# Attention and experts on one core: loads and stores handed out in pieces at two places of each step, instead of one whole load at its head

## The chip, the cores and the metric

The kernel runs on one core of one Trainium2 chip. The metric is the device time of one execution in microseconds (us). Of the core, five engines matter: PE (TensorE, matrix products and transposes), PEld (its weight loads), DVE (VectorE), ACT (ScalarE), POOL (GpSimd) and SP (SyncE), which in this part of the kernel only issues transfers. Transfers run on 16 DMA engines, which the core's queues share.

## The reference

An attention over 8 batches of 8 heads, with 512 local and 32 global positions; its output is the input of a layer of 8 experts.

```python
k_all = concat([k_g, k_l], axis=2); v_all = concat([v_g, v_l], axis=2)
out_g = sm(scale * q_g @ k_all.T) @ v_all                   # 32 global queries see all
s_ll = where(|i - j| <= 32, scale * q_l @ k_l.T, -1e9)      # 512 local queries: a band
s_lg = scale * q_l @ k_g.T                                  # ... and the 32 global keys
out_l = sm(concat([s_lg, s_ll], -1)) @ concat([v_g, v_l], 2)
x = concat([out_g, out_l], 2) as (8*544 rows, 512)
logits = x @ w_gate; tokens are given to 8 experts of 544 places each, best logits first
out[tokens of e] = max(x @ w1[e], 0) @ w2[e]
```

All is in 32-bit floats.

## The kernel before, in words

The program has three parts. Attention runs to about 226 us, the choice of the experts to about 252 us, and the eight experts fill the rest. Only the attention's transfers are touched.

**Units.** Attention is cut into 80 units. A batch has eight `Local` units (two heads, half of the sequence) and two `Glob` units (four heads' global queries), in the order of four local, one global, four local, one global; the last batch has its global units earlier. A unit has four parts, each for one or two engines: `a` are the score products on PE (S, line 139, 16 PE instructions in a unit, or line 204); `e` is the masked maximum on DVE (p, line 146, and nm, line 148) and the exponential on ACT (line 151, or 219 to 225); `c` are the transposes of the weights on PE (T, line 156 or 233) and their copy out of PSUM, by ACT (line 258) or DVE (line 260); `d` are the products with the values on PE (O, line 168 or 243) and the division on DVE (lines 171 to 176, or 246 to 250). The gate's transposes and products (lines 266, 272, 281) of the batch before are strewn between.

**Steps.** The loop runs `i` from -2 to 82. Step `i` holds `a` and `e` of unit `i+2`, `c` of unit `i` and `d` of unit `i-2`. An even step goes a, c, gate, e, d; an odd step d, c, gate, a, e. The schedule is written out by hand: each engine runs its instructions in the order in which the code calls for them.

**Transfers.** There are 32 pairs of heads. A pair has a `qk` tile (queries and keys, 704 KB, 5 buffers) and a `vw` tile (the values by windows, 1040 KB, 6 buffers). When a `qk` tile has landed, POOL spreads its queries into a `qz` tile with two copies (line 91). A batch stores four pieces of its local output, `xs`, of 128x512 floats (256 KB each), and two small ones, `xg`, of its global output (line 251). All of these are issued by SP, which does so in program order: an issue that waits holds back what stands behind it. One more transfer, the table `cf` of 512 KB for the choice of the experts, is issued by POOL, behind some of its copies.

**When a transfer goes.** At the head of each step one whole load is issued: a `vw` if fewer values than keys have been called for, else the next `qk` if it is no more than three pairs ahead. `paced` ties it to the newest `nm` of DVE (line 148), so that it goes no earlier than that. The stores of a batch's `xs` are queued in `stores`, and one goes at the end of each step, tied to nothing but its data. Beside that a load waits for its buffer.

**The program's own instructions** are moved by queue 8 of the DMA engines, which the profile lists as "instruction".

Of the kernel before, what the change touches and what calls it, by code (L numbers as in the profile page):

```python
# [65 lines left out]
def attention(ctx, tc, A, consts, xd, ident, L, nbatch, rt=None):  # L66
# [8 lines left out]

    seen, stores = [], []

    def paced(ins):
        if seen:
            tc.add_manual_dep(ins.ins if hasattr(ins, "ins") else ins, seen[-1], AFTER, reason="pace")  # L80

    def load_qk(b, p):
        t = ld.tile([128, QW + KW], F32, name="qk", bufs=5)
        z = qz[(b * NP + p) % NZ]
        paced(nc.sync.dma_start(t, A["qk"][b, p]))
        q, qk[b, p] = t[:, :QW], t[:, QW:]

        def spread(eng):
            for h in range(2):
                r = slice(64 * h, 64 * h + 64)  # L90
                eng.tensor_copy(z[r, :, h, :], q[r].rearrange("p (j i) -> p j i", i=32))  # L91
        return spread

    def load_v(b, p):
        t = ld.tile([128, 2, NW, D + 1], F32, name="vw", bufs=6)
        paced(nc.sync.dma_start(t.rearrange("p h w d -> p (h w d)"), A["vw"][b, p]))
        vw[b, p] = t

# [19 lines left out]
    spread1 = load_qk(0, 1)  # L118
    load_v(0, 0)
    nc.sync.dma_start(wg.rearrange("p a b -> p (a b)"), A["wg"])  # L120
    load_qk(0, 2)(nc.gpsimd)
    load_v(0, 1)

    class Local:
# [3 lines left out]
        def a(s):  # L128
# [6 lines left out]
            for c in range(NB):  # L135
                for r in range(2):
                    j = 8 * s.u + 2 * c + r
                    k0 = 32 * ((3 * j + 1) // 2)
                    nc.tensor.matmul(st[64 * r:64 * r + 64, c, :], z[:, j].rearrange("p h i -> p (h i)"),  # L139
                                     kw[:, k0:k0 + 128], start=True, stop=True)  # L140
            s.st = st

        def e(s):
            st, nm = s.st, s.nm
            for c in range(NB):
                nc.vector.tensor_tensor_reduce(s.p[:, c, :], st[:, c, :], mask[:, 4 * s.u + c, :], 1.0, -BIG,  # L146
                                               ALU.add, ALU.max, nm[:, c:c + 1])
            mark = nc.vector.tensor_scalar(nm, nm, -SCALE, None, op0=ALU.mult)  # L148
            seen.append(mark.ins.name if hasattr(mark, "ins") else mark.name)
            for c in range(NB):  # L150
                nc.scalar.activation(s.p[:, c, :], s.p[:, c, :], AF.Exp, bias=nm[:, c:c + 1], scale=SCALE)  # L151

        def c(s):
            t = ps.tile([128, NB, 128], F32, name="T", bufs=3)
            for c in range(NB):
                nc.tensor.transpose(t[:, c, :], s.p[:, c, :], ident)  # L156
            s.pt = wk.tile([128, NB, 128], F32, name="pt", bufs=4)
            evac(s.pt, t, bool(s.u) if s.b == nbatch - 1 and s.q == NP - 1 else None)

        def d(s):  # L160
            b, q, u = s.b, s.q, s.u
            o = ps.tile([128, 2, 2, D + 1], F32, name="O", bufs=2)
            for h in range(2):
                for k in range(2):
                    for r in range(4):
                        jj = 4 * k + r
                        lo = 64 * (jj % 2) + 32 * h
                        nc.tensor.matmul(o[32 * r:32 * r + 32, k, h, :], s.pt[:, jj // 2, lo:lo + 32],  # L168
                                         vw[b, q][:, h, 8 * u + jj, :], start=True, stop=True)
            ls = wk.tile([128, 2, 2], F32, name="ls", bufs=4)  # L170
# [8 lines left out]
    def store(b):  # L179
        for k in range(NB):  # L180
            stores.append(lambda k=k: nc.sync.dma_start(
                ap_of(xd, (b * S + SG + 128 * k) * DM, [[DM, 128], [1, DM]]), xs[b][:, k]))

    class Glob:
# [3 lines left out]
        def a(s):  # L188
# [3 lines left out]
            for part in range(2):  # L192
                for r in range(2):
# [7 lines left out]
                    else:  # L201
                        mv = t[:, 32:64]
                        dd = s.sb[64 * r:64 * r + 64]
                    nc.tensor.matmul(dd, z, mv, start=True, stop=True)  # L204

# [22 lines left out]
        def c(s):  # L228
            s.pt = wk.tile([128, 6, 128], F32, name="pgt", bufs=3)
            for lo, n in ((0, 4), (4, 2)):  # L230
                t = ps.tile([128, NB, 128], F32, name="T", bufs=3)
                for k in range(n):
                    nc.tensor.transpose(t[:, k, :], s.p[:, lo + k, :], ident)  # L233
                evac(s.pt[:, lo:lo + n], t[:, :n])

        def d(s):
# [3 lines left out]
            for k in range(6):  # L240
                for r in range(4):
                    h = 4 * g + r
                    nc.tensor.matmul(o[32 * r:32 * r + 32, :], s.pt[:, k, 32 * r:32 * r + 32],  # L243
                                     vw[b, h // 2][:, h % 2, 3 * k + 1 if k < 5 else 14, 0:D],
                                     start=(k == 0), stop=(k == 5))
            nc.vector.tensor_reduce(m[:, 6:7], m[:, 3:6], axis=AX.X, op=ALU.add)
# [117 lines left out]
    for b in range(nbatch):  # L364
# [9 lines left out]
        else:  # L374
            for k, f in enumerate(lo):
                (wide if k == 4 else turns).setdefault(s0 + 1 + (k if b == nbatch - 2 else GS[k]), []).append(f)
            if gl:
                extra.setdefault(s0 + 2, []).append(lambda b=b: load_gx(b // 4))
                for k, f in enumerate(gl):
                    (wide if k == 4 else turns).setdefault(s0 + 11 + k, []).append(f)  # L380
    nl = [3, 2]

    def pairidx(u):
        if isinstance(u, Local):
            return u.b * NP + u.q
        return u.b * NP + 2 * u.g + 1

# [3 lines left out]
    for i in range(-LA, nu + 3):  # L391
        if rt and i == 2:
            rt.load()
        if rt and i == 12:
            rt.prepare()
        if i + LA < nu:
            if i >= 0 and nl[1] < nl[0]:
                load_v(*P[nl[1]])
                nl[1] += 1
            elif nl[0] < len(P) and nl[0] <= pairidx(units[i + LA]) + 3:  # L400
                load_qk(*P[nl[0]])(nc.gpsimd)
                nl[0] += 1
        even = i % 2 == 0
# [6 lines left out]
        if 0 <= i < nu:  # L410
            units[i].c()
        for f in turns.get(i, []):
            f()
        if not even and i + LA < nu:
            units[i + LA].a()
        if i + LA < nu:
            units[i + LA].e()
            if i + LA == 0:
                spread1(nc.vector)
        if even and 2 <= i <= nu + 1:  # L420
            units[i - 2].d()
            for f in wide.get(i, []):
                f()
        for f in extra.get(i, []):
            f()
        while stores:
            stores.pop(0)()
            if i < nu - 1:
                break
        if rt and i >= nu - 8:  # L430
# [803 lines left out]
```

## Time and profile before

| | |
|---|---|
| median of three runs | 703.04 us (699.8, 703.04 and 705.38) |
| the profiled execution: its own time | 701.61 us |
| its span in the profile | 699.8 us |
| granted clock of PE, mean of the span | 0.973 |
| PE busy in the span | 656.6 us (94%), 8182 instructions, and as many weight loads |
| DVE, ACT, POOL busy | 73%, 44%, 23% |

The profile is of one execution; its parts are told in the span's own time, which begins at 0. A row that gives a wait names what the engine waited for; "issue" there means time in which it waited for nothing that the profile shows. The granted clock is a share of full speed: 1.00 is 2.4 GHz, and 0.5 is 1.2 GHz.

### The profile page before, as it was taken

Reading aid. Unit: us, or ns where it says so; the run is one execution under the profiler, and the core shown is the slowest. Engines: PE = TensorE matmul, PEld = TensorE weight load, DVE = VectorE, ACT = ScalarE, POOL = GpSimd, SP = SyncE. Lnnn points to the kernel's source line nnn. Section 1 sums busy time; section 2 is a strip of 40 time slices with the busy share of each in tenths; the row PEclk is TensorE's granted clock in tenths of the full one; section 3 lists DMA queues with packets and bytes.
Section 4 is the critical chain, followed back from the end, with each engine's and each line's share of the span. In section 5 each row is a group of like instructions: output and inputs, shape, how many; then the busy total and the mean of one; then the engine's idle time right before and its main releaser. Section 6 shows DMA issues by size and latency. Waiting matters only on the chain.

```text
span 699.8 us, 20349 instructions
## 1 busy us (share of the span) xinstructions
PE 656.6 (94%) x8182; PEld 554.1 (79%) x8182; DVE 512.1 (73%) x2073; ACT 305.6 (44%) x839; POOL 164.2 (23%) x202
## 2 busy tenths in 40 slices
PE   8989999899999259999999999999999999999996
PEld 6767886787876148978978978987987997988985
DVE  4888887888887787888997987988977871631510
ACT  4647665666665013424433332433442451642411
POOL 5231221321210041052142124132132133312011
PEclk9999999999999559999999999999999999999998
DMA  9989998998942043054144224424324324622001
GB/s 364 420 289 349 337 315 320 309 307 314 346 144 100 2 154 151 4 191 177 29 160 166 89 101 140 177 81 154 137 69 164 138 69 166 195 71 104 16 20 45
DMA packets 27102, 120.45 MB, mean 172 GB/s; under 512 B 5632, under 2 KB 5888, under 8 KB 18816
## 3 DMA queue, kind: packets, MB, share of 16 engines
q1 hardware_dynamic: 16368, 66.72, 26.2%
q0 software_dynamic: 10640, 52.44, 21.5%
q8 instruction: 64, 1.05, 0.6%
q14 instruction: 30, 0.25, 0.1%
HBM read 101.32 MB, written 17.83 MB: 170 GB/s over the span
## 4 chain that ended last, share of the span: by engine, by line
PE 85%; DVE 10%; issue 2%; ACT 1%; DMA 1%; POOLq 0%; SPq 0%; DVEq 0%; ACTq 0%
PE H L1076 27%; PE Y L1102 25%; PE S L139 8%; PE T L156 4%; PE O L168 4%; PE R L564 3%; PE Y L1092 2%; PE H L902 2%; PE S L204 2%; PE T L233 2%; PE O L243 2%; PE T L266 2%; DVE p L146 1%; DVE r_G L489 1%; DVE w1l L489 1%
## 5 line engine op out<-in xcount | busy, mean ns | idle before, releaser
L1076 PE MATMUL H<-xh,w1h 128*128 128x272 f32 (+2 forms) x512 | 149.2, 292 | 1.2 <-ACT xh L875 0.8
L1076 PE MATMUL H<-xh,w1l 128*128 128x272 f32 (+2 forms) x512 | 149.6, 293 | 0.3 <-DVE w1l L489 0.3
L1076 PE MATMUL H<-xl,w1h 128*128 128x272 f32 (+2 forms) x512 | 148.6, 291 | 0.2 <-DVE xl L489 0.2
L151 ACT ACTIVATE p<-p,nm 128x128 f32<-128x128 f32 x256 | 81.7, 391 | 63.9 <-DVE nm L148 50.7
L1102 PE MATMUL Y<-w2h,hh 128*128 128x512 f32 x256 | 104.1, 407 | 0.0
L1102 PE MATMUL Y<-w2h,hl 128*128 128x512 f32 x256 | 103.3, 403 | 0.0
L1102 PE MATMUL Y<-w2l,hh 128*128 128x512 f32 x256 | 103.3, 403 | 0.0
L1079 ACT ACTIVATE hh<-H 128x272 fp32r<-128x272 f32 (+2 forms) x128 | 50.8, 397 | 114.4 <-PE H L1076 106.9
L1076 PEld LDWEIGHTS H<-xh,w1h 128*128 128x128 f32 x512 | 96.7, 189 | 2.2 <-ACT xh L875 1.1
L1076 PEld LDWEIGHTS H<-xl,w1h 128*128 128x128 f32 x512 | 96.3, 189 | 0.8 <-DVE xl L489 0.6
L1076 PEld LDWEIGHTS H<-xh,w1l 128*128 128x128 f32 x512 | 96.6, 189 | 0.4 <-DVE w1l L489 0.4
L91 POOL COPY qz<-qk 64x544 f32<-64x544 f32 x60 | 38.2, 636 | 146.0 <-DMA qk<-in_qk_dram 82.9
L139 PE MATMUL S<-qk,qz 128*64 128x128 f32 x1024 | 68.3, 283 | 4.4 <-issue 3.2
L489 DVE SCALAR_TENSOR_TENSOR hl<-H,hh 128x272 fp32r<-128x272 f32 (+2 forms) x128 | 55.0, 435 | 20.7 <-ACT h L1081 13.2
L146 DVE CUSTOM_DVE_ANT_0 p<-S,mask 128x128 f32<-128x128 f32 x256 | 58.8, 286 | 12.7 <-PE S L139 11.7
L139 PEld LDWEIGHTS S<-qk,qz 128*64 128x64 f32 x1024 | 57.4, 141 | 11.0 <-issue 8.4
L489 DVE TENSOR_TENSOR w2l<-w2r,w2h 128x512 fp32r<-128x512 f32 x64 | 41.9, 686 | 30.5 <-ACT w2h L875 30.0
L862 POOL DMA_INDIRECT xg<-xd,idx x40 | 39.7, 992 | 101.5 <-DVE idx L489 41.0
L1038 ACT ACTIVATE y<-Y 128x512 f32<-128x512 f32 x32 | 19.1, 598 | 94.7 <-PE Y L1102 79.8
L1102 PEld LDWEIGHTS Y<-w2h,hh 128*128 128x128 f32 x256 | 48.3, 189 | 10.3 <-issue 1.6
L1102 PEld LDWEIGHTS Y<-w2h,hl 128*128 128x128 f32 x256 | 48.3, 189 | 9.2
L1102 PEld LDWEIGHTS Y<-w2l,hh 128*128 128x128 f32 x256 | 48.4, 189 | 8.9
(185 smaller groups left out, 1139.7 us busy)
## 6 DMA issues: line engine op xcount, KB each, us to landing
vw<-in_vw_dram SPq DMA_DIRECT2D x32, 1040.0 KB
qk<-in_qk_dram SPq DMA_DIRECT2D x32, 704.0 KB
xd<-xs SPq DMA_DIRECT2D x32, 256.0 KB
xg<-xd,idx POOLq DMA_INDIRECT x40
mask<-in_mask_dram SPq DMA_DIRECT2D x1, 512.0 KB
cf<-in_cf_dram POOLq DMA_DIRECT2D x1, 512.0 KB
xd<-xg SPq DMA_DIRECT2D x16, 32.0 KB
gx<-xd POOLq DMA_DIRECT2D x8, 64.0 KB
```

The lines of the kernel that those rows point to most:

```text
L91: eng.tensor_copy(z[r, :, h, :], q[r].rearrange("p (j i) -> p j i", i=32))
L139: nc.tensor.matmul(st[64 * r:64 * r + 64, c, :], z[:, j].rearrange("p h i -> p (h i)"), kw[:, k0:k0 + 128], start=True, stop=True)
L146: nc.vector.tensor_tensor_reduce(s.p[:, c, :], st[:, c, :], mask[:, 4 * s.u + c, :], 1.0, -BIG, ALU.add, ALU.max, nm[:, c:c + 1])
L151: nc.scalar.activation(s.p[:, c, :], s.p[:, c, :], AF.Exp, bias=nm[:, c:c + 1], scale=SCALE)
L156: nc.tensor.transpose(t[:, c, :], s.p[:, c, :], ident)
L168: nc.tensor.matmul(o[32 * r:32 * r + 32, k, h, :], s.pt[:, jj // 2, lo:lo + 32], vw[b, q][:, h, 8 * u + jj, :], start=True, stop=True)
L489: return op(*args, **kw)
L564: s.nc.tensor.matmul(out, *args, **kw)
L862: nc.gpsimd.indirect_dma_start(out=dst, out_offset=None, in_=src, element_offset=off, in_offset=bass.IndirectOffsetOnAxis(ap=idx, axis=0))
L1076: nc.tensor.matmul(p, w[d][:, fs], x[:, d, q], start=(k == 0), stop=(k == 11))
L1079: nc.scalar.activation(hh[:, f, q], p, AF.Relu)
L1102: nc.tensor.matmul(p, h[:, f, q], w[f], start=(f + k == 0), stop=(f + k == 9))
```

## The change

`move` takes the place of `paced`: a transfer is tied to `mark`, the newest product or transpose of PE at the place where it is called for. Stores go through `move` as well. `slot` issues at most one piece. It is called twice in each step from the first: right behind `c`, and at the end of PE's part of the step (behind `a` in an odd one, behind `d` in an even one). It takes the next `qk` if, by its own reckoning of buffers, one is free and the pair is needed no later than the next values (with a lead that favours keys by four units), else a store if more than two are queued or no values can go, else one half of a `vw`. The values so go in halves of 520 KB, one head each. Before the first step the same loads go as before, the values in two halves, and one more `qk` at the very start of the loop. A batch's two `xg` stores stand where they stood. The four lines that only note `newest[0]` in `d` and in `Glob` are left out below.

```diff
--- before.py
+++ after.py
@@ -73,16 +73,17 @@
     G = [(b, g) for b in range(nbatch) for g in range(2)]
     qk, vw, xs = {}, {}, {}
 
-    seen, stores = [], []
-
-    def paced(ins):
-        if seen:
-            tc.add_manual_dep(ins.ins if hasattr(ins, "ins") else ins, seen[-1], AFTER, reason="pace")
+    mark, newest, stores = [None], [None], []
+
+    def move(dst, src):
+        ins = nc.sync.dma_start(dst, src).ins
+        if mark[0]:
+            tc.add_manual_dep(ins, mark[0], AFTER, reason="pace")
 
     def load_qk(b, p):
         t = ld.tile([128, QW + KW], F32, name="qk", bufs=5)
         z = qz[(b * NP + p) % NZ]
-        paced(nc.sync.dma_start(t, A["qk"][b, p]))
+        move(t, A["qk"][b, p])
         q, qk[b, p] = t[:, :QW], t[:, QW:]
 
         def spread(eng):
@@ -91,10 +92,11 @@
                 eng.tensor_copy(z[r, :, h, :], q[r].rearrange("p (j i) -> p j i", i=32))
         return spread
 
-    def load_v(b, p):
-        t = ld.tile([128, 2, NW, D + 1], F32, name="vw", bufs=6)
-        paced(nc.sync.dma_start(t.rearrange("p h w d -> p (h w d)"), A["vw"][b, p]))
-        vw[b, p] = t
+    def load_v(b, p, h):
+        if h == 0:
+            vw[b, p] = ld.tile([128, 2, NW, D + 1], F32, name="vw", bufs=6)
+        n = NW * (D + 1)
+        move(vw[b, p][:, h].rearrange("p w d -> p (w d)"), A["vw"][b, p, :, h * n:h * n + n])
 
     qz = [ac.tile([128, QW // 32, 2, 32], F32, name=f"qz{i}") for i in range(NZ)]
     pg = [ac.tile([128, 6, 128], F32, name=f"pg{i}") for i in range(2)]
@@ -116,10 +118,12 @@
     nc.sync.dma_start(mask.rearrange("p a b -> p (a b)"), A["mask"])
     nc.sync.dma_start(ident, A["ident"])
     spread1 = load_qk(0, 1)
-    load_v(0, 0)
+    for h in range(2):
+        load_v(0, 0, h)
     nc.sync.dma_start(wg.rearrange("p a b -> p (a b)"), A["wg"])
     load_qk(0, 2)(nc.gpsimd)
-    load_v(0, 1)
+    for h in range(2):
+        load_v(0, 1, h)
 
     class Local:
         def __init__(s, b, u):
@@ -136,8 +140,8 @@
                 for r in range(2):
                     j = 8 * s.u + 2 * c + r
                     k0 = 32 * ((3 * j + 1) // 2)
-                    nc.tensor.matmul(st[64 * r:64 * r + 64, c, :], z[:, j].rearrange("p h i -> p (h i)"),
-                                     kw[:, k0:k0 + 128], start=True, stop=True)
+                    newest[0] = nc.tensor.matmul(st[64 * r:64 * r + 64, c, :], z[:, j].rearrange("p h i -> p (h i)"),
+                                               kw[:, k0:k0 + 128], start=True, stop=True)
             s.st = st
 
         def e(s):
@@ -145,15 +149,14 @@
             for c in range(NB):
                 nc.vector.tensor_tensor_reduce(s.p[:, c, :], st[:, c, :], mask[:, 4 * s.u + c, :], 1.0, -BIG,
                                                ALU.add, ALU.max, nm[:, c:c + 1])
-            mark = nc.vector.tensor_scalar(nm, nm, -SCALE, None, op0=ALU.mult)
-            seen.append(mark.ins.name if hasattr(mark, "ins") else mark.name)
+            nc.vector.tensor_scalar(nm, nm, -SCALE, None, op0=ALU.mult)
             for c in range(NB):
                 nc.scalar.activation(s.p[:, c, :], s.p[:, c, :], AF.Exp, bias=nm[:, c:c + 1], scale=SCALE)
 
         def c(s):
             t = ps.tile([128, NB, 128], F32, name="T", bufs=3)
             for c in range(NB):
-                nc.tensor.transpose(t[:, c, :], s.p[:, c, :], ident)
+                newest[0] = nc.tensor.transpose(t[:, c, :], s.p[:, c, :], ident)
             s.pt = wk.tile([128, NB, 128], F32, name="pt", bufs=4)
             evac(s.pt, t, bool(s.u) if s.b == nbatch - 1 and s.q == NP - 1 else None)
 
...
@@ -178,7 +181,7 @@
 
     def store(b):
         for k in range(NB):
-            stores.append(lambda k=k: nc.sync.dma_start(
+            stores.append(lambda k=k: move(
                 ap_of(xd, (b * S + SG + 128 * k) * DM, [[DM, 128], [1, DM]]), xs[b][:, k]))
 
     class Glob:
...
@@ -378,12 +381,26 @@
                 extra.setdefault(s0 + 2, []).append(lambda b=b: load_gx(b // 4))
                 for k, f in enumerate(gl):
                     (wide if k == 4 else turns).setdefault(s0 + 11 + k, []).append(f)
-    nl = [3, 2]
-
-    def pairidx(u):
-        if isinstance(u, Local):
-            return u.b * NP + u.q
-        return u.b * NP + 2 * u.g + 1
+    nl = [3, 4]
+
+    def pairs(u):
+        return [u.b * NP + u.q] if isinstance(u, Local) else [u.b * NP + 2 * u.g + r for r in range(2)]
+
+    use = [[k for k, u in enumerate(units) if n in pairs(u)] for n in range(len(P))]
+
+    def slot(i, scored, made):
+        mark[0] = newest[0].ins.name if i >= 0 else None
+        n, m = nl[0], nl[1] // 2
+        k = n < len(P) and (n < 5 or use[n - 5][-1] <= scored)
+        v = m < len(P) and (m < 6 or use[m - 6][-1] <= made)
+        if k and (not v or use[n][0] + 2 < use[m][0] + 6):
+            load_qk(*P[n])(nc.gpsimd)
+            nl[0] += 1
+        elif stores and (len(stores) > 2 or not v):
+            stores.pop(0)()
+        elif v:
+            load_v(*P[m], nl[1] % 2)
+            nl[1] += 1
 
     nu = len(units)
     first = rt.setup(slice(0, 24), True) if rt else None
@@ -393,13 +410,6 @@
             rt.load()
         if rt and i == 12:
             rt.prepare()
-        if i + LA < nu:
-            if i >= 0 and nl[1] < nl[0]:
-                load_v(*P[nl[1]])
-                nl[1] += 1
-            elif nl[0] < len(P) and nl[0] <= pairidx(units[i + LA]) + 3:
-                load_qk(*P[nl[0]])(nc.gpsimd)
-                nl[0] += 1
         even = i % 2 == 0
         if not even and 2 <= i <= nu + 1:
             units[i - 2].d()
@@ -409,10 +419,16 @@
             units[i + LA].a()
         if 0 <= i < nu:
             units[i].c()
+        if i == -LA:
+            slot(i, 0, -1)
+        if i >= 0:
+            slot(i, i + LA - (not even), i - 1 - even - 1)
         for f in turns.get(i, []):
             f()
         if not even and i + LA < nu:
             units[i + LA].a()
+            if i >= 0:
+                slot(i, i + LA, i - 2)
         if i + LA < nu:
             units[i + LA].e()
             if i + LA == 0:
@@ -421,12 +437,12 @@
             units[i - 2].d()
             for f in wide.get(i, []):
                 f()
+        if even and i >= 0:
+            slot(i, i + LA, i - 2)
         for f in extra.get(i, []):
             f()
-        while stores:
+        while stores and i >= nu:
             stores.pop(0)()
-            if i < nu - 1:
-                break
         if rt and i >= nu - 8:
             next(first, None)
 
```

**SP at the start.** In the listings `in_qk_dram` and `in_vw_dram` are the inputs, a number behind a name is that of a tile, and a tile of values in halves shows as two pieces of 128x1040. These are SP's rows from the fourth `qk` on, in the kernel before:

```order
L85 DMA qk_152<-in_qk_dram 128x1408
L96 DMA vw_198<-in_vw_dram 128x2080
L96 DMA vw_227<-in_vw_dram 128x2080
L85 DMA qk_258<-in_qk_dram 128x1408
L96 DMA vw_304<-in_vw_dram 128x2080
L85 DMA qk_354<-in_qk_dram 128x1408
L96 DMA vw_410<-in_vw_dram 128x2080
L85 DMA qk_460<-in_qk_dram 128x1408
```

and in the changed one:

```order
L79 DMA qk_165<-in_qk_dram 128x1408
L79 DMA vw_218<-in_vw_dram 128x1040 x2
L79 DMA qk_237<-in_qk_dram 128x1408
L79 DMA vw_252<-in_vw_dram 128x1040 x2
L79 DMA qk_308<-in_qk_dram 128x1408
L79 DMA vw_340<-in_vw_dram 128x1040 x2
L79 DMA qk_385<-in_qk_dram 128x1408
```

The fifth `qk` now stands ahead of the fourth values, the sixth ahead of the fifth and the seventh ahead of the sixth: each of these keys is one load of values earlier in the row. Each row with "x2" is two issues.

**SP in a batch of the middle.** Before, from one global store to behind the next:

```order
L251 DMA xd_62<-xg_1333 4x32x64
L181 DMA xd_62<-xs_855 128x512
L85 DMA qk_1419<-in_qk_dram 128x1408
L181 DMA xd_62<-xs_855 128x512
L96 DMA vw_1479<-in_vw_dram 128x2080
L181 DMA xd_62<-xs_855 128x512
L85 DMA qk_1534<-in_qk_dram 128x1408
L181 DMA xd_62<-xs_855 128x512
L96 DMA vw_1593<-in_vw_dram 128x2080
L251 DMA xd_62<-xg_1650 4x32x64
L85 DMA qk_1700<-in_qk_dram 128x1408
L96 DMA vw_1752<-in_vw_dram 128x2080
```

and now:

```order
L254 DMA xd_62<-xg_1343 4x32x64
L79 DMA vw_1360<-in_vw_dram 128x1040 x2
L79 DMA qk_1396<-in_qk_dram 128x1408
L79 DMA qk_1435<-in_qk_dram 128x1408
L79 DMA xd_62<-xs_868 128x512 x2
L79 DMA vw_1518<-in_vw_dram 128x1040 x2
L79 DMA xd_62<-xs_868 128x512 x2
L254 DMA xd_62<-xg_1662 4x32x64
L79 DMA vw_1665<-in_vw_dram 128x1040 x2
L79 DMA qk_1708<-in_qk_dram 128x1408
L79 DMA qk_1737<-in_qk_dram 128x1408
L79 DMA vw_1771<-in_vw_dram 128x1040 x2
```

Keys and values no longer alternate: two `qk` stand back to back between two `vw`, and the stores go two by two. On PE, DVE and ACT the order of the instructions is as it was.

## Rows read from the trace of the kernel before

**Rows 1.** The page: busy time with instruction counts, the instruction queue, two loads' sizes

```profile
PE 656.6 (94%) x8182; PEld 554.1 (79%) x8182; DVE 512.1 (73%) x2073; ACT 305.6 (44%) x839; POOL 164.2 (23%) x202
...
q8 instruction: 64, 1.05, 0.6%
...
vw<-in_vw_dram SPq DMA_DIRECT2D x32, 1040.0 KB
qk<-in_qk_dram SPq DMA_DIRECT2D x32, 704.0 KB
```

**Rows 2.** Windows: start:end, length, busy time (instructions) by engine, clock, DMA share, GB/s

```profile
10.00:20.00 10.00, 8.85 (x150) 6.39 (x148) 8.05 (x40) 7.11 (x24) 3.19 (x5) 1.00 1.03 428
...
60.00:80.00 20.00, 19.85 (x446) 15.85 (x448) 16.93 (x91) 13.93 (x45) 5.09 (x8) 1.00 0.92 319
80.00:100.00 20.00, 20.00 (x460) 15.68 (x458) 17.27 (x93) 13.48 (x44) 3.82 (x6) 1.00 0.96 334
...
180.00:200.00 20.00, 20.00 (x455) 15.19 (x452) 17.23 (x92) 14.06 (x46) 4.75 (x8) 1.00 0.86 313
```

**Rows 3.** Waits in 0 to 205: engine, line, cause: total, times, longest (us)

```profile
POOL qz L91 <- DMA qk<-in_qk_dram: 82.9, 18, 8.5
...
PE O L243 <- issue: 4.3, 2, 2.5
...
PE S L139 <- issue: 3.2, 3, 1.3
...
PE O L168 <- issue: 1.3, 1, 1.3
```

**Rows 4.** The chain of waits, 25 to 46: start, length, what

```profile
28.87 0.90 PE S L139 x16
...
31.16 1.33 issue
...
37.35 2.50 issue
...
40.90 1.87 PE S L139 x16
```

**Rows 5.** The chain of waits, 92 to 115

```profile
110.00 1.29 issue
```

**Rows 6.** Timeline of PE around 134: the idle time before stands in brackets

```profile
134.82 0.32 PE L243 MATMUL O<-vw,pgt 128*32 128x64 f32 x7 [1.77 <-issue]
```

**Rows 7.** Windows between those gaps, and behind the longest

```profile
32.45:39.80 7.35, 4.86 (x126) 4.09 (x125) 4.61 (x28) 4.56 (x14) 2.42 (x4) 1.00 1.01 418
111.20:134.80 23.60, 21.77 (x504) 17.74 (x505) 19.14 (x110) 15.36 (x50) 5.79 (x10) 1.00 0.88 297
...
40.90:44.40 3.50, 3.50 (x24) 2.27 (x24) 2.26 (x12) 0.17 (x1) 1.50 (x3) 0.51 0.98 323
```

**Rows 8.** DMA queues: queue 1 from 31.2 to 37.4, queue 8 from 37.4 to 38.5

```profile
q1 hardware_dynamic: 554, 2.59, 101.1%
...
q8 instruction: 1, 0.02, 5.4%
```

**Rows 9.** Timeline of SP, 12 to 34: start and length of an issue

```profile
25.53 0.33 SPq L85 DMA_DIRECT2D qk<-in_qk_dram  x1
...
29.53 0.38 SPq L85 DMA_DIRECT2D qk<-in_qk_dram  x1
```

**Rows 10.** Timeline of POOL: the copies that follow those two keys

```profile
34.39 1.33 POOL L91 COPY qz<-qk 64x544 f32<-64x544 f32 x2 [3.15 <-DMA qk<-in_qk_dram]
38.59 1.33 POOL L91 COPY qz<-qk 64x544 f32<-64x544 f32 x2 [2.88 <-DMA qk<-in_qk_dram]
```

**Rows 11.** Timeline of SP, 92 to 116

```profile
101.14 0.33 SPq L96 DMA_DIRECT2D vw<-in_vw_dram  x1
101.51 1.47 SPq L181 DMA_DIRECT2D xd<-xs  x1
103.14 0.33 SPq L85 DMA_DIRECT2D qk<-in_qk_dram  x1
103.51 0.50 SPq L181 DMA_DIRECT2D xd<-xs  x1
...
108.05 0.53 SPq L251 DMA_DIRECT2D xd<-xg  x1
```

More of the change, by code (lines that the diff above doesn't have):

```diff
@@ L167, in d @@
                         lo = 64 * (jj % 2) + 32 * h
-                        nc.tensor.matmul(o[32 * r:32 * r + 32, k, h, :], s.pt[:, jj // 2, lo:lo + 32],
-                                         vw[b, q][:, h, 8 * u + jj, :], start=True, stop=True)
+                        newest[0] = nc.tensor.matmul(o[32 * r:32 * r + 32, k, h, :], s.pt[:, jj // 2, lo:lo + 32],
+                                                   vw[b, q][:, h, 8 * u + jj, :], start=True, stop=True)
             ls = wk.tile([128, 2, 2], F32, name="ls", bufs=4)
@@ L203, in a @@
                         dd = s.sb[64 * r:64 * r + 64]
-                    nc.tensor.matmul(dd, z, mv, start=True, stop=True)
+                    newest[0] = nc.tensor.matmul(dd, z, mv, start=True, stop=True)
         def e(s):
@@ L232, in c @@
                 for k in range(n):
-                    nc.tensor.transpose(t[:, k, :], s.p[:, lo + k, :], ident)
+                    newest[0] = nc.tensor.transpose(t[:, k, :], s.p[:, lo + k, :], ident)
                 evac(s.pt[:, lo:lo + n], t[:, :n])
@@ L242, in d @@
                     h = 4 * g + r
-                    nc.tensor.matmul(o[32 * r:32 * r + 32, :], s.pt[:, k, 32 * r:32 * r + 32],
-                                     vw[b, h // 2][:, h % 2, 3 * k + 1 if k < 5 else 14, 0:D],
-                                     start=(k == 0), stop=(k == 5))
+                    newest[0] = nc.tensor.matmul(o[32 * r:32 * r + 32, :], s.pt[:, k, 32 * r:32 * r + 32],
+                                               vw[b, h // 2][:, h % 2, 3 * k + 1 if k < 5 else 14, 0:D],
+                                               start=(k == 0), stop=(k == 5))
             nc.vector.tensor_reduce(m[:, 6:7], m[:, 3:6], axis=AX.X, op=ALU.add)
```

## The prediction

> **What bounds the kernel now.** The views were read in this order: the page, the table of windows, the list of waits, then the chain of waits with the DMA view around the gaps. The page shows PE busy for 656.6 us of the span [rows 1]; since the change touches only the attention's transfers, the first question is what PE lacks before 226 us. In the windows it lacks hardly anything: 19.85, 20.00 and 20.00 us busy of 20 [rows 2]. There the time is PE's own work, and no transfer schedule shortens it. The DMA engines are nearly as full: a share of 1.03 at 428 GB/s from 10 to 20, and 0.86 to 0.96 later [rows 2]. At 428 GB/s a `vw` of 1040 KB takes 2.49 us, a half 1.25, a `qk` of 704 KB 1.68, a store of 256 KB 0.61.
>
> So I looked for what PE waits for. The list has no wait of PE for a `vw` or `qk` transfer among its larger rows; POOL waits for keys (82.9 us), but it runs far ahead of PE. PE's largest waits are put down to "issue": 4.3 us in O (line 243), 3.2 in S (line 139, nearly all of it in two gaps) and 1.3 in O (line 168) [rows 3]. The chain places four of them: 1.33 us at 31.16, 2.50 at 37.35 [rows 4], 1.29 at 110.00 [rows 5] and 1.77 before 134.82 [rows 6]. Together 6.89 us. All four lie inside a run of like products whose inputs had long been there.
>
> What they wait for is read from their distance. Between the end of the first and the start of PE's work behind the second lie 126 products and 125 weight loads; between the third and the fourth 504 and 505 [rows 7]. With a few other instructions of PE's own these are 256 and 4 x 256. Queue 8 moved 64 packets, 1.05 MB, that is 16 KB for each 256 of the 2 x 8182 instructions [rows 1]. PE stands at block ends, then, because its next block of instructions has not come. And in the DMA view between the first gap and the second, queue 8 moves nothing while queue 1 (the loads and stores) takes all of the 16 engines, 101.1%; its packet comes at once behind, inside the second gap [rows 8]. The fetch stands behind data that are queued ahead of it. The second gap has a price of its own: from 40.90 the clock granted is 0.51, the lower of the two levels (1.2 of 2.4 GHz), and S takes 1.87 us for 16 products against 0.90 at 28.87 [rows 4, 7]. Half of the 3.5 us of that window would be saved at the full clock, 1.75 us.
>
> So what the change can win is bounded: 6.89 + 1.75 = 8.6 us, 1.2%. What counts is not how early data come but **how much transfer is queued when PE asks for a block**.
>
> **The change part by part.** *PE, DVE, ACT.* Their order is unchanged, and the marks are PE's own ends of products: 0 us. PE's blocks of instructions so end at the same places in the program.
>
> *SP.* It now issues 64 halves for 32 values. An issue takes 0.33 to 0.38 us [rows 9], so 32 more cost some 11 us of SP in 226: nobody waits for SP's time itself. But SP is in order, and now its stores wait too. Behind a waiting piece stand all later loads. What this holds up is hidden by the lead of the data: the keys are copied by POOL while PE works three pairs behind. If that cover were gone, a wait of the size of one transfer (1.25 to 2.49 us) would appear at a first use; I see no place where it goes, since the lead is counted in steps of some 2.5 us and several of them.
>
> *Halves.* The bytes are the same, so the DMA time is the same at equal rate: 0 us, if the rate of a 520 KB piece is that of the whole. The trace shows 704 and 256 KB pieces beside 1040 KB ones and a share of about 1 throughout, without a loss that could be put to the small ones. Should a piece cost 4% more, the engines at 0.86 to 0.96 would still have room, except before 42.
>
> The Trainium skill speaks against this part: "DMA: Bandwidth & Descriptors", section "Measured (HBM→SBUF, 128 partitions, SWDGE, issued from GpSimd)", asks for at least 1 MiB a transfer for 75% of peak; here the mean was 419 to 428 GB/s with pieces queued back to back, and by the page's rule the values, 32 loads of 2.49 us, would take an estimated 27 us more of DMA time at three quarters of the rate, which would hit the start first.
>
> *The start.* In before a step issues one whole load: a `vw` and a `qk` by turns, 2.49 + 1.68 = 4.17 us of transfer for two steps. Now two steps issue up to four pieces, three halves and a key (3.75 + 1.68 = 5.43), until buffers bind; and each `qk` from the fifth on stands one load of values earlier in SP's row. The queue was already deep: a key issued at 25.53 was followed by POOL's copy at 34.39, one of 29.53 at 38.59 [rows 9, 10], 8.9 and 9.1 us, of which 1.68 is its own. The fetches that came late are those of 31.16 and 37.35. I count the queue in this stretch as deeper by one key, 1.68 us. Bounds: none (buffers hold the extra key back: 0), or both fetches later by it (+3.36). I take it once, **+1.7 us**, since only one of the two gaps has as full a queue just ahead of it, and the two windows are one queue apart.
>
> *The middle.* In before the densest place is from 101.14 to 103.51: a `vw`, a store, a `qk` and a store issued in 2.4 us [rows 11], 2.49 + 0.61 + 1.68 + 0.61 = 5.4 us of transfer, which leaves 3.0 us queued; the gap at 110.00 follows. Now a single step issues at most two pieces, which is gentler: two halves are 2.5 us in a step of about 2.5. But keys stand back to back, and behind an `xg` (108.05 [rows 11]), which waits for DVE's division and holds SP, two halves, two keys and two halves come in a row: 8.35 us of transfer in the three steps' 5 to 6 us, which leaves 2.3 to 3.3. The peak is what it was. That a block end meets it is chance: in before two of some 25 block ends in the middle did. So the 1.29 + 1.77 = 3.06 stay: **0 us**, with bounds of -3.06 (none meets it) and +6.1 (one in each of six batches does, at the 1.5 us that the two show in the mean: 9.2 - 3.06).
>
> *`cf`.* It goes one copy of POOL's later, 512 KB or 1.2 us of transfer moved from about 19 into the full stretch; the sum of bytes before the gaps is the same: 0 us.
>
> **Sum.** 701.61 (the profiled execution's own time: 699.8 of span and 1.8 around it) + 1.7 = 703.3. The median of the three runs is 1.43 above that execution, and a new median will be compared with it: 703.04 + 1.7 = **704.7 us**, which is no change that can be told. About 1% (7 us) is what a measurement of this kernel can tell from none: its three runs lie 5.6 us apart.
>
> **Rivals.** *The pieces let the fetch through* (faster). No more than two pieces are issued in a step, so the queue stays short, the four gaps close, and the clock does not fall behind the second: 703.04 - 8.6 = 694.4 us. For it: the stores, which before went untied straight behind a load [rows 11], now have a place of their own, and a half is half as long. Against it: the engines' share of 0.86 to 1.03 [rows 2] says that the bytes of a batch need nearly all its time, so that a queue must build wherever issue is uneven, and the start needs more, not less.
>
> The Trainium skill has a rule by which this rival would come out: "DMA: Bandwidth & Descriptors", section "Queues, rings and completion order", says that each DMA engine takes turns between its queues, packet by packet. By that rule a fetch on queue 8 would wait for a packet or two and not for loads queued on queue 1, and the gaps would not be there before either; the trace disagrees, as no packet of queue 8 passed in 6.2 us [rows 8].
>
> *The bunches starve PE more often* (slower). The mechanism is the `xg` wait on SP: pieces whose marks pass meanwhile go at once behind it, on top of back-to-back keys. If the queue then passes the 3.0 us of 101.14 at a block end in every batch, it costs 6.1 us in the middle, and 1.7 at the start: 703.04 + 7.8 = 710.8 us. It decides once six or more block ends meet the bunch. If the second gap's clock loss comes again behind one of them, 1.75 more, 712.6. For it: six pieces in a row in the listing; against it: empty slots follow, in which the queue drains.
>
> *The change does not do what it says.* SP is so far behind (buffers, `xg`) that the marks have passed when it comes to a piece, and transfers go as buffers come free, as before: the gaps stay, 703.0 us. This ends in the same class as the forecast.
>
> **How the numbers follow.** The forecast 0.40, and the change without effect 0.12: together 0.52 within 1%. The fetch let through, in the main part of its 8.6: 0.22, which is faster by over 1%. The bunches: 0.26, slower by over 1%. The range reaches from 694 (the whole gain) to 712 (a gap in each batch, and the start); what falls outside is a clock that drops in several batches, or a rate lost to the halves.
>
> **What will show it.** In the changed profile the list of waits gives PE's "issue" rows: about 8.6 us in all by the forecast, under 1 by the first rival, 13 or more by the second, and all of them whole blocks of 256 apart. The DMA view must show queue 8's packet inside each gap, and queue 1 at about 100% ahead of it. The windows from 60 to 200 must show 20.0 of 20 if the middle is free of gaps, and 0.51 in the clock only behind a gap of over 2 us. The timeline of SP must show two halves a step; if pieces go in rows without space, the change does not do what it says. A wait of PE for `vw` or `qk` would mean that the lead was no cover, and that the forecast is wrong in a way I have not priced.

## The result: 0.55% slower, and where the time went

Over 20 runs each, the median is 706.99 us against 702.96 before; the ratio is 1.0055 with a 95% interval from 1.0031 to 1.0079. That lies in the range and in the class that was forecast (within 1%), but the loss is 4.0 us and not the 1.7 of the sum. The profiled execution took 706.34 us, with a span of 704.6.

The list of waits of the changed kernel, from 12 to 225 us, answers to [rows 3]:

```profile
PE O L246 <- issue: 5.4, 5, 2.6
...
PE O L171 <- issue: 4.4, 4, 1.5
...
PE S L143 <- issue: 1.0, 2, 0.8
...
PE S L207 <- issue: 0.4, 1, 0.4
```

Together 11.2 us, where the kernel before had 6.9 in the same stretch (4.3 and 1.3 of [rows 3], and the 1.29 of [rows 5]). The difference, 4.3 us, is most of what lies between the two profiled executions (706.34 - 701.61 = 4.7 us). It is not the whole account. PE ends its last product with the values at 228.99 us, before at 223.14, so the attention takes 5.85 us longer: beside the gaps, PE's own products behind 51 us take some 2 us more in all, and why is open. Behind the attention 1.1 us come back. The chain of waits says where the gaps are (start, length, what):

```profile
76.04 1.48 issue
77.52 0.77 PE O L171 x38
...
82.59 0.30 issue
...
93.20 1.26 issue
```

None of these three stood in the kernel before, whose first gap after 50 us is that of 110.00. The gaps at the start are as they were: 1.16 us at 31.53 and 2.58 at 37.55, against 1.33 and 2.50 [rows 4]. Behind 50 us there are now ten gaps of 7.4 us in all (11.16 - 3.74), against two of 3.06. So the loss is in the middle.

The windows of the changed kernel answer to [rows 2, 7] (start:end, length, busy by engine in the order PE, PEld, DVE, ACT, POOL, then clock, DMA share, GB/s):

```profile
40.90:44.40 3.50, 3.50 (x79) 2.55 (x81) 2.82 (x13) 0.73 (x3) 2.14 (x5) 1.00 0.83 273
11.70:15.10 3.40, 3.40 (x25) 2.81 (x22) 1.27 (x10) 3.17 (x10) 1.26 (x2) 0.50 1.02 420
60.00:80.00 20.00, 18.52 (x431) 14.86 (x432) 15.98 (x88) 13.98 (x45) 4.60 (x8) 1.00 0.93 337
80.00:100.00 20.00, 18.44 (x434) 14.22 (x431) 15.35 (x85) 11.75 (x36) 3.06 (x5) 1.00 0.79 286
...
180.00:200.00 20.00, 18.94 (x431) 15.77 (x433) 16.28 (x85) 13.83 (x45) 2.55 (x4) 1.00 0.88 312
77.52:93.20 15.68, 15.38 (x378) 12.69 (x378) 12.96 (x71) 10.14 (x34) 3.04 (x5) 1.00 0.83 311
```

Three things are read here. PE, which was busy for 20.00 of 20 us from 80 to 100 and from 180 to 200, now loses 1.06 to 1.56 there. Between the end of the gap at 76 and the start of that at 93 lie 378 products and 378 weight loads, 756, which with a few other instructions of PE is 3 x 256: the gaps still stand at block ends. (Counted through the traces, with PE's semaphore instructions, all 97 gaps behind 12 us in this kernel, the one before and the variants below leave 193 or 194 when the count is divided by 256; and in each a packet of queue 8 ends 1.2 to 1.6 us before PE goes on.) And the clock's fall has moved: it is no longer at 41 (1.00, 79 products where there were 24 [rows 7]), but at 11.7, where PE has only 25 products to do.

The queue's part is seen in the DMA view, first from 72.5 to 75.2, then from 75.3 to 76.3 (packets, MB, share of 16 engines):

```profile
q1 hardware_dynamic: 236, 1.05, 100.3%
...
q8 instruction: 1, 0.02, 6.1%
```

In the first stretch queue 1 fills all the engines and no instruction packet moves; the packet then goes (75.32 to 76.30) while PE is about to stop at 76.04, and PE goes on at 77.52.

What filled queue 1 is in the timeline of SP (start, length of the issues):

```profile
57.08 0.53 SPq L254 DMA_DIRECT2D xd<-xg  x1
57.71 0.90 SPq L79 DMA_DIRECT2D vw<-in_vw_dram  x2
58.72 2.07 SPq L79 DMA_DIRECT2D qk<-in_qk_dram  x2
60.90 1.31 SPq L79 DMA_DIRECT2D vw<-in_vw_dram  x2
68.43 0.54 SPq L254 DMA_DIRECT2D xd<-xg  x1
69.06 0.89 SPq L79 DMA_DIRECT2D vw<-in_vw_dram  x2
70.33 1.39 SPq L79 DMA_DIRECT2D qk<-in_qk_dram  x2
72.36 1.79 SPq L79 DMA_DIRECT2D xd<-xs  x2
```

Behind each `xg` go two halves, two keys and two halves or stores: 8.35 us of transfer from 57.7 to 62.2, then nothing until 68.4. SP's own waits show why nothing goes ahead of them (0 to 210 us: what, total, times, longest), first in the changed kernel, then in the one before:

```profile
SPq L254 <- DVE xg L253: 40.7, 7, 7.1
SPq L254 <- DVE ls L175: 26.7, 7, 4.8
```

```profile
SPq L251 <- DVE xg L250: 12.3, 6, 7.0
...
SPq L251 <- DVE ls L172: 9.4, 7, 2.6
```

SP stands for 67 us at its `xg` stores, before for 22, while the marks of the pieces behind them pass.

What that does to queue 1 can be worked out from the traces: the bytes that SP has issued, less those that the queue's packets have moved. From 50 to 200 us the mean is 1.12 MB in both kernels. The most that is queued rose from 2.0 to 2.7 MB, and the share of the time with over 1.5 MB queued from 20 to 30%: the same bytes come in thicker bunches.

### The profile page after: what moved, and what is told of

It reads as the page before. It is cut to its first block, busy times and chain, and to the rows that moved or that the text cites. A ratio compares the mean times of both kernels' runs of the same rounds, so it can differ in the third digit from the quotient of the medians.

```text
span 704.6 us, 20423 instructions
## 1 busy us (share of the span) xinstructions
PE 655.5 (93%) x8182; PEld 553.3 (79%) x8182; DVE 512.5 (73%) x2073; ACT 306.3 (43%) x839; POOL 164.3 (23%) x202
## 3 DMA queue, kind: packets, MB, share of 16 engines
q1 hardware_dynamic: 20976, 66.72, 25.9%
## 4 chain that ended last, share of the span: by engine, by line
PE 84%; DVE 9%; issue 3%; DMA 3%; ACT 1%; POOLq 0%; SPq 0%; DVEq 0%; ACTq 0%
PE H L1092 26%; PE Y L1118 24%; PE S L143 8%; PE T L159 5%; PE O L171 4%; PE R L580 3%; PE S L207 2%; PE H L918 2%; PE Y L1108 2%; PE O L246 2%; PE T L236 2%; PE T L269 2%; DMA qk<-in_qk_dram 1%; DMA w2r<-in_w_dram,widx 1%; PE T L275 1%
## 5 line engine op out<-in xcount | busy, mean ns | idle before, releaser
L143 PEld LDWEIGHTS S<-qk,qz 128*64 128x64 f32 x1024 | 55.9, 138 | 13.3 <-issue 9.5
L1118 PEld LDWEIGHTS Y<-w2h,hh 128*128 128x128 f32 x256 | 48.4, 189 | 10.3 <-issue 1.6
```

What stands on the lines that cost most here:

```text
L143: newest[0] = nc.tensor.matmul(st[64 * r:64 * r + 64, c, :], z[:, j].rearrange("p h i -> p (h i)"), kw[:, k0:k0 + 128], start=True, stop=True)
L1118: nc.tensor.matmul(p, h[:, f, q], w[f], start=(f + k == 0), stop=(f + k == 9))
```

## The experiments

The theory after the result: PE stops at the end of a block of 256 of its instructions when the fetch of the next is late, and the fetch is late when queue 1 is full; the changed order fills it in bunches behind the `xg` wait. Rivals: the halves themselves cost; the back-to-back keys are the bunch; the gaps have nothing to do with loads. Each ratio is to the kernel before on the same chip. The gap sums are those of PE's "issue" rows from 12 to 225 us, and like the next column they are of one execution, the profiled one, whose time stands last: where it lies off the median, the gaps need not be the usual ones. The share is that of the time from 50 to 200 us with over 1.5 MB in queue 1.

| kernel | median us | ratio, 95% interval | gaps us | over 1.5 MB | profiled, us |
|---|---|---|---|---|---|
| before | 702.96 | 1 | 6.9 | 20% | 701.61 |
| changed | 706.99 | 1.0055 (1.0031 to 1.0079) | 11.2 | 30% | 706.34 |
| e1_whole | 706.65 | 1.0051 (1.0023 to 1.0079) | 8.3 | 35% | 704.22 |
| e2_halves | 703.04 | 0.9971 (0.9938 to 1.0004) | 7.5 | 13% | 703.16 |
| e3_xg_later | 703.95 | 0.9983 (0.9955 to 1.0011) | 7.9 | 18% | 704.75 |
| e4_cap | 750.90 | 1.0632 (1.0576 to 1.0688) | 2.7 | 4% | 757.24 |
| e5_cap3 | 705.72 | 1.0041 (1.0004 to 1.0077) | 8.7 | 17% | 707.46 |
| e6_later_cap5 | 704.76 | 1.0006 (0.9977 to 1.0035) | 10.1 | 16% | 707.19 |
| e7_shift | 704.13 (one run) | | 10.1 | 17% | 704.13 |
| e8_few | 696.27 | 0.9894 (0.9853 to 0.9936) | 0.5 | 0% | 695.32 |
| e9_halves_bytes | 758.85 | 1.0728 (1.0679 to 1.0776) | 0.0 | 0% | 755.38 |
| e10_later_bytes | 755.66 | 1.0706 (1.0661 to 1.0751) | 0.9 | 1% | 754.87 |
| e11_no_pair | 709.17 | 1.0049 (1.0019 to 1.0079) | 13.2 | 36% | 709.94 |
| e12_later_whole | 705.57 | 1.0024 (0.9994 to 1.0055) | 13.2 | 19% | 708.62 |

**Are the gaps the price of the loads?** `e8_few` leaves out 28 of the 32 loads of values; later pairs use those of the first four.

```diff
 def load_v(b, p):
+    n = b * NP + p
+    if n >= 4:
+        vw[b, p] = vw[P[n % 4]]
+        return
```

> The kernel before with only the first four loads of values; later pairs use the values of these four (28 of 32 loads of 1040 KB are left out, the rest of the work is the same). Theory (the fetch waits behind queued loads): with the queue nearly empty no issue gap over 0.3 us is left, the clock does not fall at 41, and the time is 693 to 697, which is what the gaps cost in all. Rival (a block end costs PE by itself, or the gaps have another cause): the four gaps stay, 700 or more.

The time fell to 0.9894, 7.5 us of 703. One gap of 0.5 us is left, more than the 0.3 that was expected, and the clock does not fall in the attention at all. Its waits of PE on "issue" at the line of `d` (O), and its windows from 60 to 120:

```profile
PE O L247 <- issue: 0.5, 1, 0.5
...
60.00:80.00 20.00, 19.85 (x452) 15.35 (x450) 16.89 (x96) 12.24 (x40) 4.32 (x7) 1.00 0.51 166
80.00:100.00 20.00, 20.00 (x456) 16.16 (x454) 16.94 (x95) 14.82 (x47) 3.82 (x6) 1.00 0.53 157
100.00:120.00 20.00, 20.00 (x461) 15.66 (x459) 17.17 (x94) 14.00 (x46) 3.81 (x6) 1.00 0.52 163
```

With the engines at a share of 0.5 PE works through. The rival of gaps that have another cause falls. The bound of the prediction on what the gaps cost, 8.6 us, lies within the interval of the 7.5 (4.5 to 10.3).

**Are they at block ends?** `e7_shift` adds `SHIFT` = 24 idle products (96 instructions of PE) to the warm-up.

```diff
+    for _ in range(SHIFT):
+        nc.tensor.matmul(wt[0:32, 0, 0:1], warm[:, 0:32], warm[:, 0:1], start=True, stop=True)
```

> The kernel before with 24 idle products more in the warm-up of PE (96 instructions with their weight loads), nothing else. Theory (PE stands at the ends of blocks of 256 of its own instructions): every issue gap of over 0.4 us again has the same remainder of 256 in PE's running count, so in the attention's own count they move 96 instructions earlier, to other products; how many of the block ends meet a deep queue may change, 3 to 11 us in all. Rival (the gaps belong to places in the attention's schedule): they stay at the same products as before, at 31, 37, 110 and 133.

The gaps moved. The list of waits has none left in the global units' O or in S, and new ones in the transposes (T, line 158) and the gate's products (T, line 274); the windows between two pairs of neighbouring gaps follow (from 107.60 to 118.62, and from 42.12 to 53.10):

```profile
PE O L170 <- issue: 6.6, 8, 1.3
...
PE T L274 <- issue: 2.4, 2, 1.5
...
PE T L158 <- issue: 1.1, 1, 1.1
```

```profile
107.60:118.62 11.02, 11.02 (x252) 8.34 (x252) 8.65 (x45) 6.64 (x22) 2.56 (x4) 1.00 0.84 286
42.12:53.10 10.98, 10.51 (x252) 8.80 (x252) 10.15 (x65) 6.91 (x23) 3.43 (x7) 1.00 0.95 353
```

Between the two lie 504 products and weight loads, twice 256 with the few others, and with the 96 new instructions counted all eleven gaps keep the remainder of 193 or 194. The schedule of the loads stayed, the places followed PE's count: they are block ends. Eleven gaps make 10.1 us here, where four made 6.9.

**The halves.** `e1_whole` takes them out of the changed kernel, `e2_halves` puts them into the one before.

```diff
         if h == 0:
             vw[b, p] = ld.tile([128, 2, NW, D + 1], F32, name="vw", bufs=6)
-        n = NW * (D + 1)
-        move(vw[b, p][:, h].rearrange("p w d -> p (w d)"), A["vw"][b, p, :, h * n:h * n + n])
+            move(vw[b, p].rearrange("p h w d -> p (h w d)"), A["vw"][b, p])
```

```diff
-        paced(nc.sync.dma_start(t.rearrange("p h w d -> p (h w d)"), A["vw"][b, p]))
+        n = NW * (D + 1)
+        for h in range(2):
+            paced(nc.sync.dma_start(t[:, h].rearrange("p w d -> p (w d)"), A["vw"][b, p, :, h * n:h * n + n]))
```

> The changed kernel with each vw as one whole load, issued where its first half stood; the place of the second half stays empty. Theory (PE stands at block ends because its instruction fetch is queued behind loads, and the changed order bunches loads behind the xg store): the same bytes come in the same bunches, so the gaps at block ends stay, 8 to 12 us in all, and the time stays at 705 to 709. Rival (the halves themselves cost: more issues on SP, a lower rate of the small pieces): the time goes back to that of the kernel before, 702 to 704.

> The kernel before with each vw issued as two halves back to back, everything else as it was. Theory (queue depth at the fetch): the same depth, so gaps of 5 to 9 us in all and a time within 2 us of before, 701 to 705. Rival (the halves cost): the whole 4 us that the change lost, 706 to 708.

Whole values leave the loss where it was (1.0051), and halves alone cost nothing (0.9971, the interval just reaches 1). The rival that halves cost falls.

**The wait of SP at `xg`.** `e3_xg_later` issues each `xg` store at the end of the next step.

```diff
-            nc.sync.dma_start(ap_of(xd, b * S * DM + 4 * g * D, [[D, 4], [DM, SG], [1, D]]), xg)
+            later.append((lambda: nc.sync.dma_start(ap_of(xd, b * S * DM + 4 * g * D, [[D, 4], [DM, SG], [1, D]]), xg)))
...
         even = i % 2 == 0
+        due, later[:] = list(later), []
...
         if even and i >= 0:
             slot(i, i + LA, i - 2)
+        for f in due:
+            f()
```

> The changed kernel with each xg store issued on SP one step later, when DVE has long made it, so that SP does not stand there while marks pass. Theory (bunches behind the xg wait make the queue deep): SP's waits at xg fall from 67 us to under 20, the gaps at block ends in the middle fall from 6.6 to under 3.5 us, the time to about 703. Rival (the back-to-back keys and values make the queue deep whether or not SP waits): gaps and time stay, 705 to 709.

The time came back to that of before (0.9983). SP's list of waits:

```profile
SPq L254 <- DVE xg L253: 7.2, 1, 7.2
...
SPq L254 <- DVE gm L215: 2.1, 4, 0.6
...
SPq L254 <- DVE ls L175: 1.5, 3, 0.5
```

These rows make 11 us, with the smaller ones 13, instead of 67. The gaps fell from 11.2 to 7.9; those behind 50 us are 3.9, a little more than the 3.5 that was expected. The share of the time with over 1.5 MB queued is back at 18%.

**The back-to-back keys.** `e11_no_pair` keeps `xg` in its place and lets no two keys follow one another.

```diff
-        if k and (not v or use[n][0] + 2 < use[m][0] + 6):
+        key, last[0] = k and not last[0] and (not v or use[n][0] + 2 < use[m][0] + 6), False
+        if key:
+            last[0] = True
```

> The changed kernel in which no two keys go in a row (a half of values or a store, if one can go, stands between them); xg stands in its old place on SP. Theory (the bunch behind the xg wait is what deepened the queue): SP still waits there, gaps stay at 9 to 12 us, time 705 to 709. Rival (back-to-back keys are the bunch): gaps fall to some 7 us, time 702 to 704.

The ratio is 1.0049, with 13.2 us of gaps; SP still stands at `xg` for 67 us (40.7, 21.8 and 4.6 in three rows), and no two keys stand side by side in its list. The back-to-back keys are not what costs the time.

**Both edits.** `e12_later_whole` has the later `xg` and whole values.

> The changed kernel with both edits: the xg store one step later, and whole values at the place of the first half. Theory (bunching is what counts, the halves are neutral): as with the later xg alone, gaps of 5 to 8 us in all and a time within 2 us of before, 702 to 706. Rival (each of the two edits takes its own part of the gaps away, as 11.3 fell to 8.6 with whole values and to 7.8 with the later xg): gaps under 5 us, time 698 to 701, a version that beats both.

Neither side was right about the gaps: 13.2 us in the profile, though the ratio (1.0024, 1.7 us) is near that of before. The profiled execution was a long one, 3 us above the median, but with the `xg` wait gone the gaps can be as long as with it. So the later `xg` does not settle how many block ends are met. With values in halves it takes the loss away (1.0055 and 0.9983, intervals apart); with whole values it is not shown to (`e1_whole` 1.0051, `e12_later_whole` 1.0024, intervals that overlap). What can be said is that the three kernels with `xg` in its old place lie at 1.0049 to 1.0055 with 30 to 36% of the time over 1.5 MB, and the two with it later at 0.9983 and 1.0024 with 18 and 19%. The gaps of single executions do not follow that share (`e7_shift`: 17% and 10.1 us): which block ends are met stays open.

**A bound on the queue.** Five kernels let each load and `xs` store wait until an earlier one has landed: the second before it (`e4_cap`, on the kernel before), the third (`e5_cap3`), the fifth (`e6_later_cap5`, on `e3`), or the newest that leaves no more than 1.7 MB queued (`e9_halves_bytes` on `e2`, `e10_later_bytes` on `e3`).

```diff
+        held = size
+        for name, n in reversed(sent):
+            if held + n > LIMIT:
+                tc.add_manual_dep(ins, name, AFTER, reason="depth")
+                break
+            held += n
+        sent.append((ins.name, size))
...
+LIMIT = 1700000
```

> The kernel before, in which each load and each xs store also waits until the transfer two before it has landed, so that never more than two are queued. Theory (the fetch waits for what queue 1 holds): the four gaps of 6.9 us go or fall below 1.5 in all, the clock does not fall at 41, and the time is 694 to 698. Rival 1 (PE stands at block ends for another reason): the gaps stay at 5 to 9 us, 702 to 705. Rival 2 (a queue of two starves the start): PE waits for keys or values before 45, and the time is 703 or more though the issue gaps are gone.

> The kernel before, in which each load and each xs store also waits until the transfer three before it has landed (three may be queued; with two the keys came late and the time was 750.9). Theory (the fetch waits behind what queue 1 holds): the queue at the start falls from 9 to about 6 us, the two gaps at 31 and 37 (3.8 us) fall to under 1.5 in all, the clock does not fall at 41, and if keys no longer come late the time is 696 to 701. Rival (any wait for a landing leaves the DMA engines idle between transfers, and the keys come late again): PE waits on POOL's copies, 705 to 730.

> The changed kernel with the xg store one step later, in which each load and xs store also waits until the piece five before it has landed. Theory: five pieces are at most some 6 us, the gaps fall to 2 to 5 us in all from 7.7, and the time to 698 to 702. Rival (keys come late): PE waits on POOL's copies, 705 or more.

> The kernel before with values in halves, and each load and xs store also waits until no more than 1.7 MB (about 4 us of transfer) would be queued. A bound by count did not help: with three whole loads (6 us) the gaps stayed at 8.7 us. Theory (the fetch waits behind queued bytes, and PE stands only if it starts later than 2.4 us before the block's end): with 4 us queued the gaps fall to 1 to 4 us in all and the time to 697 to 701, if keys are not late. Rival (the wait for a landing costs the DMA engines more than the short queue gives back): PE waits on POOL's copies of keys, or the gaps stay; 704 or more.

> The changed kernel with the xg store one step later and the same bound of 1.7 MB queued. Theory: gaps 1 to 4 us in all (7.8 without the bound), time 697 to 701. Rival (the landing waits): keys late or gaps unchanged, 704 or more.

These missed, in two ways. With three whole loads or five pieces, some 6 us, the gaps were not shorter (8.7 and 10.1 us), the one at 37 still 2.5. With 1.7 MB, some 4 us, they all but vanished: `e9_halves_bytes` has no "issue" row of PE at all, `e10_later_bytes` 0.9 us. But keys came late, and the time went to 1.07. The list of `e9_halves_bytes` from 12 to 225:

```profile
POOL qz L103 <- DMA qk<-in_qk_dram: 150.8, 23, 9.4
...
PE S L153 <- POOL qz L103: 28.6, 13, 5.9
```

PE, which behind the start never waited for a key, now waits 28.6 us in this stretch, and its clock is at the lower level for 31 us of it. `e10_later_bytes` and `e4_cap` are alike: 20.8 and 26.9 us of PE's waits for POOL's copies. The short queue goes with early fetches, but that is not shown by itself, since a PE that waits for keys also asks for its blocks less often. That keys came late is what the second rival of `e4_cap` said; it had them late before 45 us, and they were late all through (2.2 us of the 26.9 lie before 45). Whether the short queue or the wait for each landing holds the keys back is not separated.

## Why the prediction was right, and where it was not

*What bounds PE.* Right, and shown: the gaps stand at ends of blocks of 256 instructions (`e7_shift`), they go when the loads go (`e8_few`), and their worth, 8.6 us, is within the interval of the 7.5 measured. Two readings were off beside it. The 3.2 us in S are three gaps, not two: 1.29 at 110.00, and 0.96 and 0.94 before 12 us, which end as DVE's copies of the first two keys end and are no block ends (remainders 44 and 109). And the view behind [rows 8] has one row more, of another instruction queue:

```profile
q14 instruction: 1, 0.01, 0.3%
```

So an instruction packet did pass in those 6.2 us. The rows show when a packet moved, not when it was asked for; how a fetch ranks against queue 1 stays open.

*PE, DVE, ACT; SP's time; the halves.* 0 us each, as said: `e2_halves` shows no cost of the halves (0.9971), and the packets of queue 1 took 26.2% of the span before and 25.9% in the changed kernel, 183 and 182 us for the same 66.72 MB. By the rule that a transfer should have at least 1 MiB for three quarters of the peak (the Trainium skill, "DMA: Bandwidth & Descriptors", section "Measured (HBM→SBUF, 128 partitions, SWDGE, issued from GpSimd)") the halves would have taken an estimated 27 us more of DMA time; these runs disagree with it at 520 KB.

*The start, +1.7 us.* This term was mis-sized: it measured 0. The two gaps there are 3.74 us, against 3.83, although the queue was deeper (2.4 MB in the mean from 20 to 40 us, before 2.1). Nor is the one behind 37 tied to the depth as the sum took it: it was 2.5 to 2.6 us in the kernel before, in the changed one, in `e2_halves`, `e3_xg_later`, `e5_cap3`, `e6_later_cap5` and `e11_no_pair` alike, but 1.07 in `e1_whole`. Where it was 2.5 to 2.6, the packet moved 0.1 to 0.2 us after PE had stopped; why it came just then is open.

*The middle, 0 us (bounds -3.06 and +6.1).* This is the step that failed. The text had 8.35 us of transfer come in 5 to 6 us, leave 2.3 to 3.3 queued, and concluded that the peak is what it was; the number of block ends met it left to chance. The six pieces came in 4.5 us (57.71 to 62.21), which leaves 3.9 us queued, and the most that was queued rose from 2.0 to 2.7 MB. The gaps measured +4.4 (7.42 against 3.06), inside the bounds: ten instead of two, most of them short. What the step left out is what SP's 67 us at `xg` do: they squeeze the same bytes into less time. Whether the peak or the time above some depth counts, the runs do not separate. The second rival named this mechanism and asked for six block ends; ten were met, but at 0.74 us each, not 1.5. The time lies between forecast and rival, and that it lies so near the forecast is in part luck: the start came out 1.7 below its term and the middle 4.4 above.

*The clock.* The 1.75 us behind 37 were taken as the price of a gap of over 2 us. The changed kernel has a gap of 2.58 there and no fall, but one at 11.7, behind waits of PE of 1.47 and 2.03 us for DVE's copies of the first keys. So that part of the test did not hold. Nor was the price 1.75 in the end: without the fall at 41 the changed kernel gained 1.7 us on the one before by the 641st product, but its PE then waited 1.79 us for ACT's `pg` at 47, before 0.98, and by the 751st product 0.85 us of it was left.

*The other signs.* Two halves a step with space between them did not come: SP's timeline shows rows of six pieces and pauses. That is in part the rival by which the change does not do what it says: the marks had passed when SP came to a piece. Behind 12 us no wait of PE for values or keys appeared in the changed kernel, so the lead of the data was cover enough.

## What to carry to other kernels

In this kernel the gaps of a busy engine that "waits for nothing" were its instruction fetch. What told it was counting: their distances were multiples of 256 of the engine's own instructions. Their price was set by the load on the DMA engines, not by the data that PE works on. Moving loads about changed which block ends were met, by a few us in either direction, while fewer bytes took the gaps away. A queue that issues in order should not hold a small store that waits for another engine ahead of paced loads: with values in halves, SP's place for `xg` decided whether this change lost 0.55% or nothing.

## What was not expected of the hardware

None of the bounds on the queue that were tried served both the instruction fetch and the loads: at 1.7 MB queued hardly a fetch was late and the keys were (1.07), at some 6 us queued the keys were in time and the fetches late. And the granted clock did not fall behind a 2.58 us gap at 37.55 (1.00 from 40.9 to 44.4), where behind one of 2.50 at the same place it was 0.51; of the eight traces with a gap of 2.3 to 2.6 us there, six show the fall.
